# Pooling keys and values on VectorE with one strided reduce, and the keys' second copy on ScalarE

## The chip, the cores and the metric

One core of one Trainium2 chip runs the whole program. The metric is the device time of one execution in microseconds. The engines are named as in the profile: PE is TensorE, DVE VectorE, ACT ScalarE, POOL GpSimd and SP SyncE, whose queue issues the DMAs.

## The reference

Attention in which keys and values are first averaged over groups of eight positions, then two dense blocks with a gate between their matrices:

```python
B, H, S, D = 8, 8, 576, 64          # q, k, v
k_p = k.reshape(B, H, S // 8, 8, D).mean(axis=3)      # 72 pooled keys a head
v_p = v.reshape(B, H, S // 8, 8, D).mean(axis=3)
attn = softmax(q @ k_p.T / sqrt(D))
x = (attn @ v_p) as [B * S, H * D]                    # 4608 tokens of 512
h = x @ w_in;   x = (h * cos(h)) @ w_out              # w_in 512 x 2048
h = x @ w_in2;  out = (h * clip(h + 3, 0, 6) / 6) @ w_out2
```

## The kernel before

The dense blocks run token block by token block (nine blocks of 512), and in each over chunks of 128 hidden columns. Every product is made of three, since both sides are split into a high and a low part (`xh`, `xl`, `wh`, `wl`). PE does `gemm1` (line 175) and `gemm2` (line 237); ACT and DVE evict and apply the gate in between; the weights arrive as 64-bit words and are put together from them on DVE (lines 116 to 128).

Attention goes batch by batch, in units of 128 query rows, and its pieces are woven between the first steps of the dense block: the tables at the top of `tile_kernel` say how many pieces stand behind each step. A scheduler then sets the order of each engine's instructions from the order in which the program is written and from its own costs; engines run their instructions strictly in that order.

A batch's keys and values are loaded into one buffer, `raw`: 128 partitions with 5 rows of 512 words each, a row being one group of eight positions of 64 words (`load_kv`). Keys, values, the next batch's keys and so on take turns in this single buffer, so a load waits until the pooling ahead of it has read the buffer. `pool_kv` sums the eight positions. Line 334 adds halves in place, first 1280 and then 640 elements per partition; line 338 adds the last two quarters into the target, `kp` for keys and `vt` for values. For keys line 338 runs twice, as `kp` holds each pooled key in two copies next to each other. `make_kbd` transposes both copies on PE (lines 348 and 364) and ACT puts the results into a block-diagonal matrix, `kbd` (line 345), against which the scores are made (line 407). `make_v` splits `vt` on ACT and GpSimd (lines 373 to 382).

The table `VD` sends the pooling of the second batch's values to GpSimd; the other fifteen poolings run on DVE. The softmax around them takes DVE too: a maximum (line 416), a subtraction (418), a sum (429) and its reciprocal (430, 431).

Of the kernel before, what the change touches and what calls it, by code (L numbers as in the profile page):

```python
# [12 lines left out]
AF = mybir.ActivationFunctionType  # L13
ALU = mybir.AluOpType
AX = mybir.AxisListType
# [14 lines left out]
def tile_kernel(ctx, tc, q, k, v, wi1, wo1, wi2, wo2, ident_d, mask_d, out):  # L30
    nc = tc.nc
    B, H, S, D = q.shape
# [30 lines left out]
    KC = (H * SP + P - 1) // P  # L63
# [262 lines left out]
    def pool_kv(b, nm, eng, step=KC):  # L326
        kt = ap.tile([P, KC, 2, D], F32, tag="kp", name="kp") if nm == "k" else None
        vt = ap.tile([P, KC, D], F32, tag="vt", name="vt") if nm == "v" else None
        for c in range(0, KC, step):
            t = raw_t[:, c : min(c + step, KC)]  # L330
            w = POOL * D
            while w > 2 * D:
                w //= 2
                eng.tensor_tensor(  # L334
                    out=t[:, :, :w], in0=t[:, :, :w], in1=t[:, :, w : 2 * w], op=ALU.add
                )
            for o in [kt[:, c : min(c + step, KC), e] for e in range(2)] if nm == "k" else [vt[:, c : min(c + step, KC)]]:
                eng.tensor_tensor(out=o, in0=t[:, :, :D], in1=t[:, :, D : 2 * D], op=ALU.add)
        kp[b, nm] = kt if nm == "k" else vt
# [167 lines left out]
    def attention():  # L507
        units = B * NU
        normed = finished = 0
        for n in range(units + 3):  # L510
# [12 lines left out]
            if n < units and b + 1 < B:  # L523
                if i == 2:
                    pool_kv(b + 1, "k", nc.vector if KD[b + 1] else nc.gpsimd)
                    load_kv(b + 1, "v")
                if i == 4:
                    make_kbd(b + 1, 0)
                    yield
                    make_kbd(b + 1, 1)  # L530
                    yield
# [3 lines left out]
            while finished < normed and n - finished >= 2:  # L535
                unit_pt(finished)
                yield
                qb, qi = divmod(finished, NU)
                finished += 1
                if qi in (1, 3):  # L540
                    unit_pt_rest(qb, qi - 1)
                    yield
                for part, (u0, u1) in enumerate(PARTS[qb]):
                    if qi == min(u1 - 1 + (part == 0) * PV0, NU - 1):
                        for j in range(NP):
                            pv(qb, part, j)
                            yield
                        if UNITS[u1 - 1][0] + P >= N:
                            started.append(qb)
                if qi == NU - 1:  # L550
                    done.append(qb)
                    if qb + 1 < B:
                        pool_kv(qb + 1, "v", nc.vector if VD[qb + 1] else nc.gpsimd)
                        make_v(qb + 1)
                        if qb + 2 < B:
                            load_kv(qb + 2, "k")
# [22 lines left out]
    for t in vr.values():  # L579
        nc.gpsimd.memset(f(t), 0.0)  # L580
    pool_kv(0, "k", nc.vector, K0S)
    load_kv(0, "v")
    make_kbd(0, 0)
# [77 lines left out]
    for slot in range(2 * (T + LAG) + 4):  # L661
# [3 lines left out]
        if not odd and s < T:  # L665
# [9 lines left out]
            if key[0] == 1 and fc == NF - 5:  # L675
                for c in range(NC):
                    t = ypl.tile([P, N], F32, tag="yv", name="yv", bufs=4)
                    nc.sync.dma_start(
                        out=t, in_=yp_d[c * P : (c + 1) * P, bl * N : (bl + 1) * N]
# [6 lines left out]
            if nxt < T:  # L686
                nm, nk, nbl = steps[nxt][:3]
# [87 lines left out]
```

## Time and profile before

| | us |
|---|---|
| median of three runs | 1803.48 |
| lowest and highest | 1799.16 and 1804.42 |
| the profiled execution | 1801.62 |
| its span | 1799.8 |
| PE busy in it | 1739.2 (97%) |
| DVE busy | 896.4 (50%) |
| ACT busy | 891.6 (50%) |
| POOL busy | 393.8 (22%) |

A share of busy time is a mean over stages that differ: attention fills roughly the first 440 us, with dense work in it from about 87 us on, and behind it the dense blocks run alone. What a change in attention is worth is read from the stretch in which it lies.

### The profile page before, as it was taken

The page shows a single profiled execution, that of the slowest core. Times are in us where ns is not written, and L with a number is a line of the kernel's source. Part 1 is how long each engine was busy: PE and PEld are TensorE (multiplying, and loading weights), DVE is VectorE, ACT ScalarE, POOL GpSimd, SP SyncE. Part 2 cuts the span into 40 slices and gives each one's busy share as a digit, 9 for nine tenths or more (in the row PEclk, how much of TensorE's full clock was granted, in tenths as well). Part 3 has the DMA queues.
Part 4 walks back from the last instruction along what each step waited for, and adds up shares of the span by engine and source line. Part 5 has one row for each costly group of instructions (what it writes and reads, how often), then busy time and mean ns, then how long its engine had stood idle before and what let it go on. Part 6 is the DMA issues. An engine that isn't in the chain of part 4 may idle for free.

```text
span 1799.8 us, 21002 instructions
## 1 busy us (share of the span) xinstructions
PE 1739.2 (97%) x7952; PEld 1429.5 (79%) x7952; DVE 896.4 (50%) x1398; ACT 891.6 (50%) x1508; POOL 393.8 (22%) x320
## 2 busy tenths in 40 slices
PE   5689999999999999999999999999999999999999
PEld 4567777788888888888888788888888888888887
DVE  6998656656777656654446852222222222222222
ACT  3588878787666655555556543232323222232222
POOL 2755444222223222221112421010101000010000
PEclk7799999999999999999999999999999999999999
DMA  7656442323333313222223411010101010100000
GB/s 196 194 172 195 143 136 74 118 83 103 117 105 118 106 59 105 97 85 76 71 70 106 140 59 47 1 47 1 47 1 48 0 47 8 40 18 24 0 24 24
DMA packets 115077, 139.84 MB, mean 78 GB/s; under 512 B 44192, under 2 KB 68896, under 8 KB 114976
## 3 DMA queue, kind: packets, MB, share of 16 engines
q1 hardware_dynamic: 114976, 138.51, 24.8%
q8 instruction: 62, 1.02, 0.2%
q14 instruction: 39, 0.32, 0.1%
HBM read 100.73 MB, written 37.75 MB: 77 GB/s over the span
## 4 chain that ended last, share of the span: by engine, by line
PE 85%; DVE 6%; DMA 3%; POOL 2%; ACT 2%; issue 2%; SPq 0%; DVEq 0%; POOLq 0%; ACTq 0%
PE y L237 40%; PE h L175 40%; PE ap_ps L494 1%; PE ap_ps L407 1%; DVE raw L334 1%; DMA raw<-in_k_dram 1%; DMA raw<-in_v_dram 1%; POOL xl L153 1%; DVE sm L429 1%; DVE g L196 1%; POOL e L433 1%; DVE a L125 1%; PE ap_ps L393 0%; PE ap_ps L459 0%; DVE sm L430 0%
## 5 line engine op out<-in xcount | busy, mean ns | idle before, releaser
L175 PE MATMUL h<-xl,wh 128*128 128x512 f32 x1152 | 451.3, 392 | 4.2 <-POOL xl L153 4.2
L175 PE MATMUL h<-xh,wh 128*128 128x512 f32 x1152 | 453.5, 394 | 0.5 <-DVE g L209 0.5
L175 PE MATMUL h<-xh,wl 128*128 128x512 f32 x1152 | 450.8, 391 | 0.0
L201 DVE SCALAR_TENSOR_TENSOR g<-g,h 128x512 f32<-128x512 f32 x144 | 99.3, 689 | 454.7 <-ACT g L187 454.7
L153 POOL TENSOR_TENSOR xl<-xr,xh 128x512 fp32r<-128x512 f32 x108 | 153.3, 1438 | 779.2 <-ACT xh L152 778.1
L187 ACT ACTIVATE g<-h,bias_c 128x512 f32<-128x512 f32 x144 | 99.0, 687 | 409.7 <-PE h L175 409.3
L218 DVE TENSOR_TENSOR gl<-g,gh 128x512 fp32r<-128x512 f32 x255 | 190.3, 746 | 157.7 <-ACT gh L212 154.4
L212 ACT ACTIVATE gh<-g 128x512 fp32r<-128x512 f32 x288 | 181.6, 630 | 175.2 <-DVE g L201 104.5
L175 PEld LDWEIGHTS h<-xl,wh 128*128 128x128 f32 x1152 | 216.7, 188 | 50.2 <-POOL xl L153 6.5
L175 PEld LDWEIGHTS h<-xh,wh 128*128 128x128 f32 x1152 | 216.9, 188 | 45.5 <-issue 1.2
L175 PEld LDWEIGHTS h<-xh,wl 128*128 128x128 f32 x1152 | 216.9, 188 | 44.3
L237 PE MATMUL y<-gh,wh 128*128 128x512 f32 x576 | 226.7, 394 | 0.0
L237 PE MATMUL y<-gl,wh 128*128 128x512 f32 x576 | 226.6, 393 | 0.0
L237 PE MATMUL y<-gh,wl 128*128 128x512 f32 x576 | 225.6, 392 | 0.0
L237 PE MATMUL y<-wh,gh 128*128 128x512 f32 x576 | 224.3, 389 | 1.1 <-DVE yv L245 1.1
L237 PE MATMUL y<-wh,gl 128*128 128x512 f32 x576 | 224.1, 389 | 0.0
L237 PE MATMUL y<-wl,gh 128*128 128x512 f32 x576 | 224.1, 389 | 0.0
L196 DVE SCALAR_TENSOR_TENSOR g<-g,t 128x512 f32<-128x512 f32 x144 | 112.6, 783 | 149.8 <-ACT g L195 149.5
L134 POOL TENSOR_TENSOR wl<-a,wh 128x512 fp32r<-128x512 f32 x64 | 88.4, 1381 | 269.4 <-ACT wh L133 269.4
L237 PEld LDWEIGHTS y<-wh,gh 128*128 128x128 f32 x576 | 108.2, 188 | 24.4 <-DVE yv L245 1.9
L199 ACT ACTIVATE g<-g 128x512 f32<-128x512 f32 x144 | 91.0, 632 | 72.9 <-DVE g L196 72.5
L237 PEld LDWEIGHTS y<-wh,gl 128*128 128x128 f32 x576 | 108.1, 188 | 22.5
(110 smaller groups left out, 2086.1 us busy)
## 6 DMA issues: line engine op xcount, KB each, us to landing
xr<-x_d SPq DMA_DIRECT2D x72, 256.0 KB, 3.2
st<-in_moe_w_in_dram SPq DMA_DIRECT2D x32, 512.0 KB, 6.6
st<-in_moe_w_out_dram SPq DMA_DIRECT2D x32, 512.0 KB, 4.1
yp_d<-ys SPq DMA_DIRECT2D x36, 256.0 KB, 2.4
yv<-yp_d SPq DMA_DIRECT2D x36, 256.0 KB, 3.4
xr<-y_d SPq DMA_DIRECT2D x36, 256.0 KB, 2.7
out_dram<-ys SPq DMA_DIRECT2D x36, 256.0 KB, 2.0
raw<-in_k_dram SPq DMA_DIRECT2D x8, 1024.0 KB, 5.7
```

What stands on the lines that cost most here:

```text
L125: nc.vector.scalar_tensor_tensor(out=a, in0=hi, scalar=0xC0000000, in1=a, op0=ALU.bitwise_and, op1=ALU.bitwise_or)
L134: nc.gpsimd.tensor_tensor(out=wl, in0=w, in1=f(wh), op=ALU.subtract)
L153: nc.gpsimd.tensor_tensor(out=xl, in0=t, in1=f(xh), op=ALU.subtract)
L175: nc.tensor.matmul(h, a[:, cs], z, start=(n == 0), stop=(n == 3 * NC - 1))
L187: nc.scalar.activation(out=g, in_=hs[s], func=AF.Relu, bias=bias_c[:, 2:3], scale=1.0)
L196: mark[s] = nc.vector.scalar_tensor_tensor(out=g, in0=g, scalar=MAGIC, in1=t, op0=ALU.subtract, op1=ALU.subtract)
L199: nc.scalar.activation(out=g, in_=g, func=AF.Sin, scale=-TWO_PI)
L201: mark[s] = nc.vector.scalar_tensor_tensor(out=g, in0=g, scalar=6.0, in1=h, op0=ALU.min, op1=ALU.mult)
L212: nc.scalar.activation(out=gh, in_=g, func=AF.Copy)
L218: eng.tensor_tensor(out=gl, in0=gs[s][0], in1=f(gh), op=ALU.subtract)
L237: nc.tensor.matmul(y[c], a, z, start=(first and n == 0), stop=(last and n == 2))
L334: eng.tensor_tensor(out=t[:, :, :w], in0=t[:, :, :w], in1=t[:, :, w : 2 * w], op=ALU.add)
```

## The change

In `pool_kv`, poolings on DVE become one reduce over a view of `raw` in which the eight positions are the innermost dimension. Neighbours in that dimension are 64 words apart. For keys it writes the first copy in `kp`, and ACT copies it to the second. The branch for GpSimd stays as it was. `raw` is no longer written by the pooling. Behind the change line numbers are 8 higher than before.

```diff
         for c in range(0, KC, step):
             t = raw_t[:, c : min(c + step, KC)]
+            if eng is nc.vector:
+                o = kt[:, c : min(c + step, KC), 0] if nm == "k" else vt[:, c : min(c + step, KC)]
+                eng.tensor_reduce(
+                    out=o, in_=t.rearrange("p c (r d) -> p c d r", d=D), op=ALU.add, axis=AX.X
+                )
+                if nm == "k":
+                    nc.scalar.activation(out=kt[:, c : min(c + step, KC), 1], in_=o, func=AF.Copy)
+                continue
             w = POOL * D
             while w > 2 * D:
```

`KC` is 5 and `step` is 5 everywhere, so each pooling is one reduce. The order of instructions changes on all engines through the first 440 us. Three places show how.

On DVE at the start of the program, the first batch's keys and values; before:

```order
L334 TENSOR_TENSOR raw<-raw 128x5x256
L334 TENSOR_TENSOR raw<-raw 128x5x128
L338 TENSOR_TENSOR kp<-raw 128x5x64 x2
L416 TENSOR_REDUCE mx<-ap_ps 128x4 x2
L418 TENSOR_TENSOR e_96<-ap_ps,mx 128x288 x2
L416 TENSOR_REDUCE mx<-ap_ps 128x4
L334 TENSOR_TENSOR raw<-raw 128x5x256
L429 TENSOR_REDUCE sm<-e_96 128x8
L334 TENSOR_TENSOR raw<-raw 128x5x128
L430 TENSOR_SCALAR sm<-sm 128x8
L418 TENSOR_TENSOR e_97<-ap_ps,mx 128x288
L338 TENSOR_TENSOR vt<-raw 128x320
```

The same place after the change:

```order
L333 TENSOR_REDUCE kp<-raw 128x5x64
L424 TENSOR_REDUCE mx<-ap_ps 128x4 x2
L426 TENSOR_TENSOR e_96<-ap_ps,mx 128x288 x2
L333 TENSOR_REDUCE vt<-raw 128x320
L437 TENSOR_REDUCE sm<-e_96 128x8
```

Four instructions for the keys have become one, and three for the values, which had two of the softmax between them, one that runs ahead of the softmax's sum.

On DVE, the pooling of the fourth batch's values, among steps of the softmax and of the gate (`g`); before:

```order
L334 TENSOR_TENSOR raw<-raw 128x5x256
L209 TENSOR_TENSOR g<-h,g 128x512
L334 TENSOR_TENSOR raw<-raw 128x5x128
L429 TENSOR_REDUCE sm<-e_97 128x8
L464 TENSOR_TENSOR ptl<-ap_ps,pth 128x4x128
L430 TENSOR_SCALAR sm<-sm 128x8
L472 TENSOR_TENSOR pth<-ap_ps,pth 64x256
L431 RECIPROCAL sm<-sm 128x8
L338 TENSOR_TENSOR vt<-raw 128x320
```

And after:

```order
L209 TENSOR_TENSOR g<-h,g 128x512
L125 SCALAR_TENSOR_TENSOR a<-st,a 128x512
L116 TENSOR_SCALAR a<-st 128x512
L128 SCALAR_TENSOR_TENSOR a<-e,a 128x512
L437 TENSOR_REDUCE sm<-e_99 128x8
L333 TENSOR_REDUCE vt<-raw 128x320
L438 TENSOR_SCALAR sm<-sm 128x8
L472 TENSOR_TENSOR ptl<-ap_ps,pth 128x4x64
```

The reduce stands in one piece and earlier: at the softmax's sum over `e_99`, where the three sums stood around that over `e_97` (four buffers take turns, so that is two units on). `raw` comes free there.

On ACT, around the third batch's keys; before:

```order
L502 ACTIVATE xs<-y_548 128x320
L379 ACTIVATE vml<-spl,mask 128x4x64
L395 ACTIVATE qT<-ap_ps 128x512
L463 ACTIVATE pth<-ap_ps 128x4x128
L152 ACTIVATE xh<-xr 128x512 x2
L395 ACTIVATE qT<-ap_ps 128x4x64
L423 ACTIVATE e_96<-e_96 128x576
```

And after:

```order
L387 ACTIVATE vml<-spl,mask 128x4x64 x2
L403 ACTIVATE qT<-ap_ps 128x512
L337 ACTIVATE kp<-kp 128x5x64
L510 ACTIVATE xs<-y_542 128x320
L471 ACTIVATE pth<-ap_ps 128x4x128
L403 ACTIVATE qT<-ap_ps 128x4x64
L431 ACTIVATE e_96<-e_96 128x576
```

The copy of the keys (line 337) has come in ahead of an eviction (`xs`), of transposed probabilities (`pth`), of transposed queries (`qT`) and of an exponential, and the copies `xh` have moved behind them.

## Rows read from the trace of the kernel before

**Rows 1.** the page's part 2, PE busy in tenths, 40 slices of 45 us

```profile
PE   5689999999999999999999999999999999999999
```

**Rows 2.** stretches: limits, length, busy of each engine, clock, DMA share, GB/s

```profile
20.00:160.00 140.00, 107.78 (x518) 84.53 (x519) 131.07 (x218) 90.90 (x174) 82.68 (x70) 0.83 0.64 182
160.00:340.00 180.00, 170.57 (x901) 137.09 (x900) 120.49 (x215) 145.07 (x252) 76.81 (x72) 1.00 0.45 137
340.00:440.00 100.00, 98.82 (x528) 80.88 (x527) 58.16 (x117) 83.55 (x143) 28.37 (x27) 1.00 0.23 73
440.00:1800.00 1360.00, 1355.00 (x5977) 1121.08 (x5975) 579.67 (x835) 567.11 (x931) 204.70 (x147) 1.00 0.18 57
```

**Rows 3.** same columns, DVE on `raw` alone, a stretch per pooling; last all

```profile
7.00:11.00 4.00, 3.21 (x4) 1.00 0.99 155
20.00:25.00 5.00, 2.79 (x3) 0.86 0.48 97
32.00:39.00 7.00, 4.21 (x4) 0.50 0.65 147
67.00:73.00 6.00, 4.10 (x4) 0.92 0.83 250
85.00:99.00 14.00, 5.02 (x3) 0.88 0.22 67
111.00:121.00 10.00, 3.60 (x4) 1.00 0.45 127
133.00:141.00 8.00, 4.07 (x3) 1.00 0.44 131
151.00:158.00 7.00, 3.17 (x4) 1.00 0.49 172
...
5.00:345.00 340.00, 54.03 (x53) 0.93 0.54 158
```

**Rows 4.** instructions of four lines: ns min/median/max, first and last start, shapes

```profile
L334 DVE TENSOR_TENSOR raw<-raw x30: 778/1478/2549, 7.4 to 332.5; 128x1280 f32<-128x1280 f32 x15, 128x640 f32<-128x640 f32 x15
...
L429 DVE TENSOR_REDUCE sm<-e x40: 734/748/756, 21.7 to 426.2; 128x8 f32<-128x576 f32 x32, 64x8 f32<-64x576 f32 x8
...
L116 DVE TENSOR_SCALAR a<-st x64: 410/421/1517, 26.2 to 1060.9; 128x512 uint32<-128x512 uint32 x64
...
L373 ACT ACTIVATE sph<-vt x8: 454/462/471, 24.0 to 349.3; 128x320 fp32r<-128x320 f32 x8
```

**Rows 5.** DVE's groups by shape: count, busy us, mean ns, idle before, releasers

```profile
L416 DVE TENSOR_REDUCE mx<-ap_ps 128x4 f32<-128x288 f32 x64 | 28.5, 452 | 28.6 <-PE ap_ps L407 28.2
...
L334 DVE TENSOR_TENSOR raw<-raw 128x1280 f32<-128x1280 f32 x15 | 25.6, 1704 | 11.7 <-DMA raw<-in_k_dram 6.3 <-DMA raw<-in_v_dram 5.4
L429 DVE TENSOR_REDUCE sm<-e 128x8 f32<-128x576 f32 x32 | 24.0, 750 | 23.4 <-ACT e L423 20.3 <-POOL gl L218 3.1
```

**Rows 6.** chain of waits from the start: start, length, what

```profile
7.36 1.50 DVE raw L334
...
8.89 0.83 DVE raw L334
...
9.75 0.91 DVE kp L338 x2
...
11.80 8.40 DMA raw<-in_v_dram
```

**Rows 7.** PE's waits to 170 us: us in total, times, longest

```profile
PE h L348 <- DVE kp L338: 13.2, 2, 10.7
PE ap_ps L407 <- DVE e L418: 10.6, 5, 4.5
```

**Rows 8.** ACT's table loads in the groups by shape

```profile
L199 ACT ACT_TABLE_LOAD x28 | 35.9, 1283 | 0.5
L423 ACT ACT_TABLE_LOAD x27 | 34.6, 1283 | 1.6 <-DVE e L418 1.1
...
L345 ACT ACT_TABLE_LOAD x1 | 1.3, 1283 | 2.4 <-DVE kbd L577 2.4
```

## The prediction

> **What bounds the kernel now.** I read the page's slices first, then the stretches, then the pools one by one. [rows 1] is to show where TensorE (PE) waits: its row is full from the fourth slice on and low only in the first three, which are 45 us each. [rows 2] gives that in numbers: from 440 us to the end PE is busy 1355.0 of 1360 us, so nothing that the change touches can be gained or lost there. PE is idle 32.2 us from 20 to 160, 9.4 us from 160 to 340 and 1.2 us in the 100 us after that. From 20 to 160 us VectorE (DVE) is busy 131.07 of 140 us, more than any other engine. There DVE sets the pace, with GpSimd (POOL, 82.68 us) as the next in its chains. From 160 to 340 us DVE is busy only 120.49 of 180 us and PE 170.57: there most of DVE's work is hidden. The granted TensorE clock is below full only in the DVE-bound stretch (0.83 in the mean), when PE has little to do; I price no term on it, since PE is not what ends late there.
>
> **What the pools cost now.** [rows 3] has one stretch for each pool and only the instructions on the buffer raw. I call them k0, v0, k1 and so on, by batch. k0, v0, k1, k2, v2, k3, v3 and k4 lie ahead of 160 us and take 3.21 + 2.79 + 4.21 + 4.10 + 5.02 + 3.60 + 4.07 + 3.17 = 30.17 us of DVE. All fifteen on DVE take 54.03 us (last row), so the seven later ones 23.86 us. v1 is on GpSimd before and after. The undisturbed price is that of k0, 3.21 us, and v0, 2.79 us. The rest is contention: k0's first sum takes 1.50 us on the chain [rows 6], the slowest 2549 ns [rows 4].
>
> **The new reduce.** One reduce reads all 2560 elements of each partition once. DVE has two reduces in the trace: 288 elements in 452 ns (from PSUM) and 576 in 750 ns (from SBUF) [rows 5]. That is (750 − 452) / 288 = 1.035 ns per element, so 2560 elements would take 0.750 + 1984 × 1.035 ns = 2.80 us. This is the lower end. The reduce of 576 elements stays between 734 and 756 ns in all forty [rows 4], in the same stretches in which the two-input sums swing, so I give the new one no contention of its own. But those reduces read neighbouring words. The new one walks `p c d r`: each next element lies 64 words (256 bytes) away. The widest step of a long DVE read in the trace is 8 bytes, the weights' words at line 116, which run at 421 ns for 512 elements at the median [rows 4]; a wider one has a handful of elements at most, and tells nothing. For the upper end I take the slowest pace at which DVE was seen to read words for this same pooling: 2549 ns for 1280 elements, 1.99 ns each [rows 4], and so 2560 × 1.99 ns = 5.10 us. Below nothing is excluded: an element more per cycle than the rows of reduces show has no row.
>
> Which end? By operation and count the nearest row is the reduce; by what is in doubt, whether a word comes in every cycle, it is the slow sum. I choose the slow end, 5.10 us, as a judgement on the step alone, with somewhat better than even odds.
>
> The Trainium skill (SBUF — State Buffer, section "Door 1: The DMA port swizzle") says that SBUF has lines of 16 bytes, that two accesses must fall in a line for full bandwidth, and that fp32 may step four elements free; this speaks against the change, as no two neighbours of the new read share a line. The trace's 8-byte step agrees and shows nothing of 256 bytes. The page gives no size; if it were a halved pace, an estimate from that page is 0.75 + 1.984 × 2.07 = 4.9 us, about my slow end, and if it costs nothing the sum is that of the first rival.
>
> **Sum at 5.10 us.** Ahead of 160 us: 8 × 5.10 − 30.17 = +10.6 us of DVE work. DVE has just 9 us idle of the 140 there, so it can hide little; against that, parts of the chain run through GpSimd, which a DVE with fewer two-input sums disturbs less. I let 0.8 of it reach the end: +8.5 us. k0 and v0 pass in full, as [rows 6] shows: load, sums, the issue of the next load, that load and v0's sums follow each other on the chain. Later: 7 × 5.10 − 23.86 = +11.8 us, in a stretch where DVE idles a third and PE is 95% busy; I let 0.2 pass: +2.4 us.
>
> **ScalarE's copy.** Eight copies of 320 elements; ScalarE (ACT) copies the same size in 462 ns at the median at line 373 [rows 4], so 3.7 us of ACT work. From k2 on at least fourteen rows of ACT's order lie between a copy and the first use of what is made from it, and ACT is busy 145.07 of 180 us even where it is fullest [rows 2]: nothing. k0 and k1 are bare: PE waits for them at line 348, 10.7 us and 2.5 us (13.2 in two) [rows 7], and now waits for reduce, copy and a hand-over: 0.46 + about 0.1 us each, +1.2 us in all. DVE's second add, 0.48 us, is in the sums above. Only the sine (line 199), the exponential (line 423) and the very first instruction of ACT load a table before [rows 8]; the copy adds none, and the first load moves ahead of k0's copy, under the input's load: nothing.
>
> **What the new order moves.** The scheduler places one reduce near where the first of the three sums stood, so raw comes free and the next load goes out earlier (before, k3's three sums stretch over 10 us, v2's over 14 [rows 3]). DVE waited 11.7 us in all for raw's loads [rows 5], the very first load among it, which stays; what else there is lies mostly behind 200 us, where DVE has time. I count no gain; the most would be 11.7 × 0.2 = 2.3 us. ACT has 52 table loads in the new order against 56. Each takes 1283 ns [rows 8], 5.1 us of ACT work less. ACT is not the bound, but few of its waits are loose; I take a tenth, −0.6 us rounded up, with bounds 0 and −5.1. Everything else that changes places (a sum of softmax, a weight step, a GEMM step a few rows earlier or later) I price at nothing, plus or minus 3 us: a stall of PE behind such a step (scores, line 407, behind the subtraction, line 418) was 2.1 us in the mean and 4.5 at most [rows 7], and they can come or go singly.
>
> Total: 8.5 + 2.4 + 1.2 − 0.6 = +11.5 us. The profiled execution took 1801.62 us (span 1799.8, and 1.8 us around it, which stay), which gives **1813 us**. That execution lies 1.9 us under the median of the three times, 1803.48, and I make no further shift for it. A measurement of this kernel can tell about 0.3% (5.4 us) from no change.
>
> **Rivals.**
> *The reduce runs at full pace (ends on the other side).* Mechanism: DVE reads a word per cycle whatever the step. Price 2.80 us; the point from which it decides is 30.17 / 8 = 3.77 us per pool, below which DVE has less to do in its full stretch. Ahead of 160 us: 8 × 2.80 − 30.17 = −7.8 us, of which I let only 0.6 pass, since POOL and the loads take over as what is late: −4.7. Later: 7 × 2.80 − 23.86 = −4.3 us × 0.2 = −0.9. With the copy and the tables: 1801.6 − 4.7 − 0.9 + 1.2 − 0.6 = 1797 us. For it speaks that both reduces run at one element per cycle and a steady time; against it the step that they do not have.
>
> *ACT is held up by its copies.* ACT runs in order, and the copy waits for DVE's reduce at a place that was chosen ahead of time. Behind k2's copy stand the eviction xs, the transposed probabilities pth, qT and an exponential, all of which feed PE. If DVE is late by some 2 us at five of the seven copies that is up to 10 us, of which half may reach PE. At full pace this takes back the gain: 1797 + 5 = 1802 us; on the slow price it makes 1818. For it: DVE has no slack before 160 us. Against: only k2, k3 and k4 have their copies there.
>
> *The change does next to nothing*: the price is near 3.8 us per pool, and DVE's sum stays. 1801 to 1803 us. A pace of 1.4 ns per element would do that; no row points to it.
>
> **How the numbers follow.** Slow reduce 0.57: its own range is 1804 to 1824 us, the upper end with all 22.4 us passing (1801.6 + 22.4 + 1.2 − 0.6 = 1825, rounded down), the lower with a fifth of the early work and none of the later. Of it 0.49 is slower by over 0.3%, 0.08 within. Full pace 0.25: 1790 to 1800, of it 0.15 faster, 0.10 within. ACT held up 0.10: 1799 to 1819, of it 0.06 slower, 0.04 within. Next to nothing 0.08: 0.04 within, 0.02 to either side, for the order. Together: faster 0.17, same 0.26, slower 0.57. The range goes from 1794 to 1824: it takes in most of the full-pace case, and leaves out some 0.1 below and less above.
>
> **What would show it.** Mean of the new DVE group at line 333: near 5.1 or near 2.8 us. DVE's busy sum: +22 us at the slow price (less the contention that goes), −12 us at the full one. k0's last sum ends at 10.66 us now [rows 6]: PE's first matmul on kp 2.5 us later than that, or within 0.3 us. If the reduce is slow and the time still falls, the share that passes is wrong, and the early stretch was not DVE's. If it is fast and the time does not fall, the next thing late (POOL, the loads, ACT's copies) has taken the gain, and PE's waits will name it.

## The result, and the profile after

The changed kernel takes 1825.54 us in the median of four runs (1822.3 to 1826.16), the kernel before 1801.69 us in four. The ratio is 1.0134, with a 95% interval of 1.0121 to 1.0146: 1.3% slower, some 24 us. The sign was forecast; the size was about twice the +11.5 us of the sum, and the time lies just above the range.

From the page of the changed kernel, busy times of the engines, PE's slices as in [rows 1], and the granted clock by slices:

```profile
PE 1747.2 (96%) x7952; PEld 1436.4 (79%) x7952; DVE 918.4 (50%) x1360; ACT 890.1 (49%) x1512; POOL 384.2 (21%) x320
...
PE   4687899999999999999999999999999999999999
...
PEclk8789999999999999999999999999999999999999
```

PE's busy time went from 1739.2 to 1747.2 us for the same 7952 matmuls, and its idle time from 60.6 to 77.1 us (span 1824.3 less busy time). So 16.5 us of the span's 24.5 are new idle time, and 8.0 us are the same work done more slowly. This division holds for these two traces only: e7 below takes the same time as the changed kernel with PE busy 1741.4 us.

The stretches that answer to [rows 2], same columns:

```profile
20.00:160.00 140.00, 103.19 (x484) 81.05 (x483) 132.57 (x192) 84.85 (x168) 75.19 (x67) 0.80 0.62 179
160.00:340.00 180.00, 162.68 (x837) 130.95 (x836) 121.33 (x182) 131.82 (x233) 68.81 (x69) 0.97 0.39 119
340.00:440.00 100.00, 95.92 (x503) 78.76 (x502) 61.23 (x113) 80.52 (x136) 27.16 (x26) 0.98 0.27 86
440.00:1800.00 1360.00, 1358.32 (x6014) 1123.38 (x6013) 589.96 (x855) 582.48 (x960) 211.86 (x153) 1.00 0.18 59
```

PE is idle 36.8 us from 20 to 160 us (32.2 before), 17.3 us from 160 to 340 (9.4) and 4.1 us from 340 to 440 (1.2). DVE's share is hardly higher anywhere: it is busy 121.33 of 180 us in the later stretch, a third idle as before. The granted clock, full in both later stretches before, is now 0.97 and 0.98.

The new group at line 333, in ns min/median/max with first and last start, and DVE's whole busy time on `raw` (columns as in [rows 3]):

```profile
L333 DVE TENSOR_REDUCE kp<-raw x8: 4452/4702/4812, 7.0 to 331.7; 128x320 f32<-128x2560 f32 x8
L333 DVE TENSOR_REDUCE vt<-raw x7: 4479/4648/4726, 21.8 to 353.6; 128x320 f32<-128x2560 f32 x7
```

```profile
5.00:375.00 370.00, 69.85 (x15) 0.91 0.50 146
```

One reduce takes 4.45 to 4.81 us. The fifteen take 69.85 us against 54.03 [rows 3]: +15.8 us of DVE, and 24 us of time.

### The profile page after: what moved, and what is told of

Same layout as the page of the kernel before. It is cut to its first block, busy times and chain, and to the rows that moved or that the text cites. A ratio compares the mean times of both kernels' runs of the same rounds, so it can differ in the third digit from the quotient of the medians.

```text
span 1824.3 us, 20961 instructions
## 1 busy us (share of the span) xinstructions
PE 1747.2 (96%) x7952; PEld 1436.4 (79%) x7952; DVE 918.4 (50%) x1360; ACT 890.1 (49%) x1512; POOL 384.2 (21%) x320
## 4 chain that ended last, share of the span: by engine, by line
PE 84%; DVE 8%; ACT 3%; issue 2%; DMA 1%; POOL 1%; SPq 0%; DVEq 0%; ACTq 0%; POOLq 0%
PE h L175 40%; PE y L237 40%; PE ap_ps L502 2%; DVE kp L333 2%; PE ap_ps L415 1%; DMA raw<-in_v_dram 1%; DVE vt L333 1%; DVE sm L437 1%; ACT L431 1%; DVE a L125 1%; DVE a L128 1%; PE ap_ps L401 1%; DVE sm L438 0%; DVE g L196 0%; DVE ptl L472 0%
## 5 line engine op out<-in xcount | busy, mean ns | idle before, releaser
L237 PEld LDWEIGHTS y<-wh,gh 128*128 128x128 f32 x576 | 108.2, 188 | 24.3 <-DVE yv L245 1.9
L237 PEld LDWEIGHTS y<-gh,wh 128*128 128x128 f32 x576 | 109.0, 189 | 22.1 <-ACT ys L253 0.5
```

Of the source, the lines that this page charges most:

```text
L237: nc.tensor.matmul(y[c], a, z, start=(first and n == 0), stop=(last and n == 2))
```

## The experiments

Theory A: the step of the read makes the reduce dear, and its extra time reaches the end wherever it lies. Rivals: the new order and the copies queued on ACT (B), the 320 short outputs (C), the length of one block on DVE (D). Each ratio is to the kernel before on the same chip; a difference of two ratios times 1800 us gives microseconds, good to about 3 us each.

**e1: the same order, neighbouring words.**

```diff
-                    out=o, in_=t.rearrange("p c (r d) -> p c d r", d=D), op=ALU.add, axis=AX.X
+                    out=o, in_=t.rearrange("p c (d r) -> p c d r", d=D), op=ALU.add, axis=AX.X
```

> The changed kernel with one thing altered: the reduce sums eight neighbouring words instead of eight words 256 bytes apart, so it pools the wrong elements. Every engine's order of instructions is exactly that of the changed kernel. Theory A (the step of the read is the cost, and it reaches the end): one reduce takes 2.8 us instead of 4.65, DVE has 28 us less to do than in the changed kernel, and the time is 1795 to 1803 us. Theory B (the new order and the copy's waits on ACT are most of the loss): the reduce takes 2.8 us too, but the time stays above 1808 us. Theory C (the 320 short outputs are the cost, not the step): the reduce stays at 4.6 us and the time at 1825 us.

Measured: 1796.51 us, ratio 0.998 (0.9971 to 0.999). DVE's groups in e1 by shape (busy us, mean ns, idle before):

```profile
L333 DVE TENSOR_REDUCE kp<-raw 128x320 f32<-128x2560 f32 x8 | 22.5, 2814 | 7.4 <-DMA raw<-in_k_dram 4.2 <-PE ap_ps L372 3.2
L333 DVE TENSOR_REDUCE vt<-raw 128x320 f32<-128x2560 f32 x7 | 19.7, 2817 | 5.4 <-DMA raw<-in_v_dram 4.1 <-issue 1.3
```

C falls: the outputs are the same and a reduce takes 2.82 us. B falls too, as the main cause: with this very order, and with the copies where they are, the kernel is 0.2% faster than before. From e1 to the changed kernel nothing differs but the step, and the traces have the same order of instructions on every engine; the step costs 15 × 1.85 = 27.6 us on DVE (69.85 against 42.2 us) and (1.0134 − 0.998) × 1800 = 27.7 us of time.

**e2: one duration for each step.**

```diff
+                st = {2: 1, 3: 2, 4: 4, 5: 8, 6: 16, 7: 32}.get(b)
+                if nm == "v" and st is not None:
+                    eng.tensor_reduce(
+                        out=vt.rearrange("p c d -> p (c d)").rearrange("p (x s) -> p x s", s=st),
+                        in_=raw_t.rearrange("p c e -> p (c e)").rearrange("p (x r s) -> p x s r", r=POOL, s=st),
+                        op=ALU.add, axis=AX.X,
+                    )
+                else:
```

> The changed kernel, in which the values of batches 2 to 7 are reduced with steps of 1, 2, 4, 8, 16 and 32 words (4 to 128 bytes) instead of 64, so those sums are of the wrong elements; keys and the first values keep 64. One duration for each step, all for 2560 elements into 320. A line of 16 bytes as the limit: 2.8 us at 1 and 2 words, 4.65 us from 4 words on, and nothing in between. A cost that grows with the step: durations rise from 2.8 towards 4.65 us over the six. No effect of the step: all near 4.65 us.

Measured in a single execution, 1823.22 us. The six reduces of e2 in order of time, so with steps of 1, 2, 4, 8, 16 and 32 words (start, us, shapes):

```profile
94.07 2.80 DVE L335 TENSOR_REDUCE vt<-raw 128x320 f32<-128x2560 f32 x1
...
123.38 2.81 DVE L335 TENSOR_REDUCE vt<-raw 128x320 f32<-128x2560 f32 x1
...
172.04 4.71 DVE L335 TENSOR_REDUCE vt<-raw 128x320 f32<-128x2560 f32 x1
...
223.95 4.84 DVE L335 TENSOR_REDUCE vt<-raw 128x320 f32<-128x2560 f32 x1 [1.81 <-DMA raw<-in_v_dram]
...
279.83 4.54 DVE L335 TENSOR_REDUCE vt<-raw 128x320 f32<-128x2560 f32 x1 [0.47 <-DMA raw<-in_v_dram]
...
350.47 4.78 DVE L335 TENSOR_REDUCE vt<-raw 128x320 f32<-128x2560 f32 x1 [0.52 <-DMA raw<-in_v_dram]
```

2.80 and 2.81 us at steps of 4 and 8 bytes, 4.54 to 4.84 us at 16 to 128 bytes, and no duration in between. It is a threshold between 8 and 16 bytes, not a slope; 12 bytes was not run. The Trainium skill (SBUF — State Buffer, section "Door 1: The DMA port swizzle") puts the limit at a line of 16 bytes with at least two hits in it. The runs agree with that: a step of 8 bytes leaves two hits in a line, a step of 16 only one. The same passage says that fp32 may step four elements free. That is not borne out here if it means a step of four, which takes 4.71 us.

**e3: the copy alone.** Pairwise sums as before; only the second copy goes to ACT.

```diff
-            for o in [kt[:, c : min(c + step, KC), e] for e in range(2)] if nm == "k" else [vt[:, c : min(c + step, KC)]]:
-                eng.tensor_tensor(out=o, in0=t[:, :, :D], in1=t[:, :, D : 2 * D], op=ALU.add)
+            o = kt[:, c : min(c + step, KC), 0] if nm == "k" else vt[:, c : min(c + step, KC)]
+            eng.tensor_tensor(out=o, in0=t[:, :, :D], in1=t[:, :, D : 2 * D], op=ALU.add)
+            if nm == "k":
+                nc.scalar.activation(out=kt[:, c : min(c + step, KC), 1], in_=o, func=AF.Copy)
```

> One half of the change alone: the pairwise sums stay as in the kernel before, but the keys' second copy is made by ACT. Theory A (the reduce's price is the loss): within 3 us of the kernel before, or up to 5 us faster, as DVE has 8 x 0.48 to 0.6 us less to do. Theory B (ACT held up by the copies): 5 to 12 us slower than the kernel before.

Measured: 1800.25 us, ratio 1.0005 (0.9995 to 1.0014). DVE on `raw` in e3 (the first columns as in [rows 3]; one memset of half a microsecond is among the 46):

```profile
0.00:345.00 345.00, 50.20 (x46) 0.94 0.54 159
```

DVE has about 4 us less to do, and the time does not move. The copy on ACT, with the add that it replaces on DVE, is neither a gain nor a loss.

**e7: the change, with DVE's own copy.**

```diff
-                    nc.scalar.activation(out=kt[:, c : min(c + step, KC), 1], in_=o, func=AF.Copy)
+                    nc.vector.tensor_copy(out=kt[:, c : min(c + step, KC), 1], in_=o)
```

> The changed kernel, but the keys' second copy is made by DVE behind its reduce, as in the kernel before; the step stays 256 bytes. Order changes slightly. If ACT's copies, queued behind the late reduces, carry part of the loss: 3 to 10 us faster than the changed kernel. If the reduce alone does: the same, or up to 5 us slower for eight more DVE instructions of about 0.4 us in the full stretch, 1825 to 1831 us.

Measured: 1826.16 us, ratio 1.015 (1.0135 to 1.0165). In e7, DVE's groups:

```profile
L333 DVE TENSOR_REDUCE kp<-raw 128x320 f32<-128x2560 f32 x8 | 37.5, 4686 | 10.9 <-PE ap_ps L372 6.4 <-DMA raw<-in_k_dram 4.5
...
L337 DVE COPY kp<-kp 128x320 f32<-128x320 f32 x8 | 2.8, 347 | 0.0
```

With 2.8 us more on DVE and no copy on ACT it is as slow as the changed kernel: ACT's copies carry nothing of the loss that shows within some 3 us.

**e5 and e6: the step early or late, in the same order.** The view is the strided one for `b < 4` in e5 and for `b >= 4` in e6, and neighbouring words otherwise.

> In the changed kernel's exact order, keys and values of batches 0 to 3 are reduced at the 256-byte step, the eight reduces of batches 4 to 7 over neighbouring words (wrong elements). Seven reduces cost 7 x 1.85 = 13.0 us more of DVE than with all of them over neighbouring words (1796.5 us). Theory A (all of it reaches the end, wherever it lies): 1808 to 1811 us. The prediction's shares (0.8 of the early work, 0.2 of the late): 1806 to 1808 us.

> The reverse, in the same order: batches 4 to 7 at the 256-byte step, batches 0 to 3 over neighbouring words (wrong elements). Eight reduces cost 8 x 1.85 = 14.8 us more of DVE, in stretches where DVE is busy two thirds of the time. Theory A (all of it reaches the end): 1809 to 1814 us. The prediction's share of 0.2 for the late stretch: 1799 to 1801 us. If neither kernel's loss adds up with the other's to 29 us, the two meet in a wait that both lengthen.

Measured: e5 1808.5 us, ratio 1.0049 (1.0034 to 1.0064); e6 1812.93 us, ratio 1.0075 (1.0058 to 1.0092). Against e1's ratio, e5 loses (1.0049 − 0.998) × 1800 = 12.4 us for 13.0 us of DVE work, e6 17.1 us for 14.8. Together 29.5 us, as much as the whole step costs within the errors: the two add. The early share is 0.95, where 0.8 was forecast; the late share is not 0.2 but about 1 (1.15, good to 0.2).

**e10: only the late values.**

```diff
-                    out=o, in_=t.rearrange("p c (r d) -> p c d r", d=D), op=ALU.add, axis=AX.X
+                    out=o, in_=t.rearrange("p c (r d) -> p c d r" if b >= 4 and nm == "v" else "p c (d r) -> p c d r", d=D), op=ALU.add, axis=AX.X
```

> The changed kernel's exact order; the 256-byte step only for the values of batches 4 to 7, neighbouring words (wrong elements) for all else: 4 x 1.85 = 7.4 us more of DVE than with neighbouring words throughout (1796.5 us). If every late reduce costs alike: 1804 to 1805 us, half of the 16.4 us that the eight cost. If the values' reduces, which stand between the softmax's maximum and the subtraction that frees the scores, carry most of it: 1806 to 1810 us. If the keys' do: below 1802 us.

Measured: 1807.76 us, ratio 1.0046 (1.0031 to 1.0061): (1.0046 − 0.998) × 1800 = 11.9 us for 4 × 1.85 = 7.4 us of DVE. Late values lose more than they take. The late keys were not run alone; 17.1 − 11.9 = 5.2 us are left for their equal 7.4, which the errors don't tell from all of it.

The place shows in the trace. DVE in the changed kernel around the fifth batch's values (start, us, line; idle before and releaser in brackets), and PE at the same time:

```profile
222.07 0.46 DVE L424 TENSOR_REDUCE mx<-ap_ps 128x4 f32<-128x288 f32 x1 [0.99 <-PE ap_ps L415]
224.63 4.54 DVE L333 TENSOR_REDUCE vt<-raw 128x320 f32<-128x2560 f32 x1 [2.10 <-DMA raw<-in_v_dram]
229.10 0.45 DVE L426 TENSOR_TENSOR e<-ap_ps,mx 128x288 f32<-128x288 f32 x1
```

```profile
225.62 0.39 PE L237 MATMUL y<-gh,wl 128*128 128x512 f32 x1
229.65 1.08 PE L401 MATMUL ap_ps<-ident,qm 128*128 128x128 f32 x4 [3.64 <-issue]
```

And in e1, DVE and PE at the same place of the program:

```profile
203.99 0.46 DVE L424 TENSOR_REDUCE mx<-ap_ps 128x4 f32<-128x288 f32 x1 [1.00 <-PE ap_ps L415]
206.58 2.82 DVE L333 TENSOR_REDUCE vt<-raw 128x320 f32<-128x2560 f32 x1 [2.14 <-DMA raw<-in_v_dram]
209.32 0.45 DVE L426 TENSOR_TENSOR e<-ap_ps,mx 128x288 f32<-128x288 f32 x1
```

```profile
207.51 0.39 PE L237 MATMUL y<-gh,wl 128*128 128x512 f32 x1
209.87 0.63 PE L401 MATMUL ap_ps<-ident,qm 128*128 128x128 f32 x4 [1.97 <-issue]
```

DVE waits 2.10 us for the load with the subtraction of line 426 queued behind the reduce. PE has 3.7 us of other matmuls behind the scores, to 226.0 us, and then runs dry; its transposes of line 401 start 0.10 us after the subtraction has ended (229.10 + 0.45, then 229.65; in e1 209.32 + 0.45, then 209.87). The trace names no releaser for them, so that they wait for the scores' buffer which this subtraction reads is inferred: from the equal 0.10 us, and from the kernel, which has two `ap_ps` buffers here, both taken by the two halves of the scores. PE stands 3.64 us with the step and 1.97 us without, 1.67 us apart for a reduce that is 1.72 us longer. PE's waits of this kind from 160 to 360 us (total, times, longest), in e10 and then in e1:

```profile
PE ap_ps L401 <- issue: 7.3, 3, 3.3
```

```profile
PE ap_ps L401 <- issue: 2.7, 2, 2.0
```

Then the clock. Four stretches of 4 us in the changed kernel around that stall, with one of 1 us listed last, and three in e1 around its own (columns as in [rows 2], granted clock third from the end):

```profile
222.00:226.00 4.00, 4.00 (x20) 3.06 (x19) 1.82 (x2) 0.89 (x2) 1.29 (x1) 1.00 0.22 76
226.00:230.00 4.00, 0.36 (x3) 0.39 (x3) 3.97 (x4) 0.63 (x1) 0.00 (x0) 0.93 0.01 2
230.00:234.00 4.00, 4.00 (x18) 3.49 (x17) 1.61 (x3) 3.19 (x4) 0.00 (x0) 0.65 0.92 279
234.00:238.00 4.00, 4.00 (x20) 3.31 (x19) 2.25 (x6) 3.30 (x7) 2.69 (x3) 1.00 0.40 88
...
230.00:231.00 1.00, 1.00 (x6) 0.90 (x5) 1.00 (x2) 0.23 (x1) 0.00 (x0) 0.50 0.62 68
```

```profile
203.50:207.50 4.00, 4.00 (x22) 3.40 (x21) 1.38 (x2) 0.40 (x2) 1.28 (x1) 1.00 0.20 59
207.50:211.50 4.00, 2.03 (x15) 1.42 (x14) 3.69 (x5) 1.93 (x4) 0.00 (x0) 1.00 0.19 35
211.50:215.50 4.00, 4.00 (x20) 3.30 (x19) 1.52 (x4) 3.96 (x6) 0.98 (x1) 1.00 1.06 331
```

Behind the stall of 3.64 us, in which PE did 0.36 us of work in 4 us, the granted clock falls: it reads 0.50 at first, the lower level of 1.2 GHz, and 0.65 over the next 4 us is a mix of that with the full 2.4 GHz, while in e1, with a stall of 1.97 us, it stays at full. So the step costs 1.7 us of stall at this place and, by estimate, 4 × (1 − 0.65) = 1.4 us of slow matmuls behind it. From 160 to 440 us in e1, e6 and e10:

```profile
160.00:440.00 280.00, 269.59 (x1430) 218.75 (x1429) 174.34 (x311) 224.96 (x391) 95.69 (x94) 1.00 0.35 109
```

```profile
160.00:440.00 280.00, 259.55 (x1358) 209.96 (x1357) 180.41 (x300) 213.38 (x368) 93.20 (x92) 0.98 0.32 98
```

```profile
160.00:440.00 280.00, 263.28 (x1378) 213.44 (x1377) 177.91 (x301) 217.66 (x376) 95.39 (x95) 0.98 0.33 101
```

PE is idle 10.4 us in e1, 20.4 in e6 and 16.7 in e10; the clock of 0.98 in the other two takes, by estimate, another 280 × 0.02 = 5.6 us, good to 1.4 us since the clock is rounded. That makes some 15.6 us for e6 (17.1 measured) and 11.9 for e10 (11.9, closer than the estimate can claim).

**e4, e8 and e9: five pieces.** Each reduce becomes five, between which the scheduler may put other work; e8 is the same order over neighbouring words, e9 takes the step for `b >= 4` alone.

```diff
+                for i in range(KC):
                     eng.tensor_reduce(
-                        out=o, in_=t.rearrange("p c (r d) -> p c d r", d=D), op=ALU.add, axis=AX.X
+                        out=o[:, i], in_=t[:, i].rearrange("p (r d) -> p d r", d=D), op=ALU.add, axis=AX.X
                     )
```

> The changed kernel with each reduce split into five, one for each row of 512 words, so that the scheduler may put other work between them; the read step stays 256 bytes. Theory D (a 4.65 us block on DVE stalls what stands behind it, beyond its work): 5 to 12 us faster than the changed kernel, though DVE's work grows by the fixed cost of four more instructions a pooling, about 0.1 us each. Theory A (the work alone counts): the same or up to 6 us slower than the changed kernel, 1825 to 1832 us.

> The kernel of five pieces with the read step taken away: neighbouring words are summed (wrong elements), in exactly that kernel's order. A piece of 512 elements should fall from 1.05 to about 0.69 us, 75 x 0.36 = 27 us less of DVE, the same saving as between the changed kernel and its contiguous form, which moved the time by 29 us. Theory A (DVE's work passes in full, in whatever portions): 1788 to 1792 us. Theory D (part of the 29 us came from the length of the block, and in short pieces DVE's work is partly hidden): a smaller share, 15 to 21 us, 1796 to 1802 us.

> The kernel of five pieces in its exact order, with the 256-byte step only for batches 4 to 7 and neighbouring words (wrong elements) for batches 0 to 3. It puts a number on the late work when other work can go between the pieces: 40 pieces, 40 x 0.375 = 15.0 us more of DVE than with all pieces over neighbouring words (1795.4 us). With blocks of 4.65 us the same late work cost 16.4 us. Theory A (late work passes in any portion): 1809 to 1812 us. Theory D (the length of the block matters late): 1801 to 1806 us. The prediction's 0.2: 1798 us.

Measured: e4 1816.9 us, ratio 1.0093 (1.0078 to 1.0108); e8 1795.42 us, ratio 0.9969 (0.9958 to 0.9981); e9 1805.11 us, ratio 1.0033 (1.0022 to 1.0044). The pieces in e4, then in e8:

```profile
L334 DVE TENSOR_REDUCE kp<-raw 128x64 f32<-128x512 f32 x40 | 40.6, 1050 | 8.1 <-PE ap_ps L373 4.1 <-DMA raw<-in_k_dram 4.0
...
L334 DVE TENSOR_REDUCE vt<-raw 128x64 f32<-128x512 f32 x35 | 35.5, 1048 | 3.8 <-DMA raw<-in_v_dram 3.8
```

```profile
L334 DVE TENSOR_REDUCE kp<-raw 128x64 f32<-128x512 f32 x40 | 25.5, 673 | 7.7 <-DMA raw<-in_k_dram 3.9 <-PE ap_ps L373 3.8
...
L334 DVE TENSOR_REDUCE vt<-raw 128x64 f32<-128x512 f32 x35 | 22.6, 676 | 6.8 <-DMA raw<-in_v_dram 6.8
```

e4 has some 6 us more on DVE than the changed kernel and is 0.4 of a percent faster: the length of the block matters, as D had it. From e8 to e4 the step costs 75 × 0.37 = 28 us of DVE and (1.0093 − 0.9969) × 1800 = 22 us of time, a share of 0.8, between what A and D expected; e8's median missed both ranges. Late alone, e9, it is 11.5 us for 15.0, where whole blocks lost 17.1 for 14.8. PE's stalls at the transposes (line 402 there) are nearly gone in e9, where e6 has 7.8 us; more of its waiting is now for ACT ahead of the scores:

```profile
PE ap_ps L416 <- ACT xs L511: 4.7, 4, 2.6
...
PE ap_ps L402 <- issue: 1.1, 2, 0.9
```

So A is right for most of the work, and D for some of the rest: the 5.6 us between e6 and e9 go with the length of the block, and with another order, and are hardly more than the errors.

## Why the prediction was right and wrong

- **The sign, and its cause:** right. The step of the read is the cost, shown by e1 and e2, and the choice between the two ends fell on the right one.
- **The price:** 5.10 us forecast from the slowest sum in [rows 4], 4.66 us measured (69.85 / 15). This term was 0.44 us too dear a pooling, and the pooling's growth on DVE +15.8 us instead of +22.4. That it came so close is in part luck: the row was a sum over neighbouring words, which takes 1.50 us elsewhere [rows 6], so its slowness was not that of a step. DVE's busy sum on the page did grow by 22.0 us (896.4 to 918.4), the sign that the prediction had named, but only 15.8 of them are pooling.
- **The price and the shares together:** two errors worked against each other. With the measured price the prediction's terms are 8 × 4.66 − 30.17 = +7.1 us early and 7 × 4.66 − 23.86 = +8.8 us late, and its shares, copy and tables make that +8.0 us. Even with both shares at 1 it is +16.5 us, where +24 was measured. The range's upper end let all of DVE's growth pass; more than all of it did.
- **The full-pace rival:** 2.80 us a reduce and 1797 us were forecast; e1 has 2.82 us and 1796.51 us. The slope from the two reduces of [rows 5] was good to 1%, and so was the absence of contention.
- **The early share, 0.8:** a little low. e5 passes 12.4 of 13.0 us, and its 1808.5 us lie in the range of theory A, half a microsecond above that of the prediction's shares (its seven reduces are those of `b < 4`; the sum counted an eighth, k4, ahead of 160 us, which is in e6).
- **The late share, 0.2:** the step that failed. It was read from busy shares ([rows 2]: DVE idle a third of the stretch, PE 95% busy), as though DVE's idle time could take the work. It can't: e6 shows 17.1 us lost for 14.8, so late work was worth some five times what the sum gave it. Of DVE's 59.5 us idle from 160 to 340 us in the kernel before, 46.5 are waits for ACT and PE, and ACT in its turn waits 9.7 us there for DVE (lines 209 and 196): the engines hand work round a loop. DVE's waits (us, times, longest):

```profile
DVE g L196 <- ACT g L195: 12.8, 8, 3.7
DVE sm L429 <- ACT e L423: 12.1, 9, 2.2
DVE g L209 <- ACT g L199: 11.4, 12, 2.8
DVE mx L416 <- PE ap_ps L407: 10.2, 11, 2.6
```

And at the place shown above PE had 3.7 us of other work to go on with, less than the wait for the load and the reduce together.
- **The clock, priced at nothing:** wrong for the late stretch. [rows 2] has it at full there; it comes down behind longer stalls (e1 against e10). Summed over stretches of 1 us, PE's busy time multiplied by what the clock lacks is 19.4 us up to 160 us and nothing from there to 460 us in the kernel before, 21.1 and 6.5 us in the changed one: so by this estimate most of the 8.0 us that PE's busy time grew by is late.
- **ScalarE's copy:** priced +1.2 us for two bare waits. The first rose from 10.7 [rows 7] to 12.0 us, reduce and copy together, where a first matmul 2.5 us after 10.66 had been forecast; the two waits together stay at 13.2:

```profile
PE h L356 <- ACT kp L337: 13.2, 2, 12.0
```

- **ACT held up by its copies:** it cost nothing that shows. ACT does stand 16.0 us for the reduces, ahead of five of its eight copies and 9.5 of them at the start, but e3 and e7 show no price for it. What was held up was DVE's own queue, by the reduce; the prediction had looked for a queue behind the wait on ACT and not behind the reduce.
- **The new order:** −0.6 us for the table loads and nothing else, plus or minus 3. In e1 the order, the copies and a reduce of 2.82 us together make −3.4 us against the 1799.9 us of the kernel before, where the rival's sum had −5.0. No run has the order alone, so that it is worth nothing isn't shown.
- **The old sums, taken as worth what the new work is worth:** the sum priced only the difference of the two, and this too failed. The step's 27.6 us on DVE cost 27.7 us of time; the 11.8 us that go from DVE between the kernel before and e1 (54.03 to 42.2 us) gave back 3.4 us. So 27.7 − 3.4 = 24.3 us are lost, for a difference on DVE of 15.8. Why the old sums were worth so little stays open. They may have been partly hidden, as three or four short instructions a pooling; or the new order costs up to some 8 us. Two runs speak for the first without showing it. e8, in pieces, has 5.9 us more on DVE than e1 and is no slower (0.9969 against 0.998). And e3, with the old sums, has DVE's busy time from 20 to 160 us down from 131.07 [rows 2] to 123.96 us, and gains nothing:

```profile
20.00:160.00 140.00, 109.33 (x536) 87.36 (x536) 123.96 (x215) 94.00 (x181) 86.72 (x71) 0.84 0.65 187
```

Left open, too: how much of a late stall would stay if the reduce stood behind the subtraction instead of ahead of it; no kernel moved it alone. No version that computes the reference was faster than the kernel before: e3 is equal to it, and e1 and e8, which are 0.2 and 0.3% faster, add neighbouring words in place of the eight rows.

## What to carry to other kernels

Count the read step of a VectorE instruction as part of its price: an fp32 reduce over a view that steps 256 bytes took 1.66 times what it took over neighbouring words, and from 16 bytes on it was about as dear. The pairwise sums over neighbouring words, 3.6 us a pooling (54.03 / 15), were cheaper than one such reduce of 4.66 us. An engine that is busy two thirds of a stretch isn't thereby able to hide more work: look at what stands behind the longer instruction on its queue, and how many microseconds of other work the engine that waits for it has in hand. Don't price a change by the difference of old and new work on one engine alone: 11.8 us less gave 3.4 us here, 27.6 us more cost 27.7. Two kernels in exactly the same order, with the one price changed, told in a single run what the step was worth, and what all the rest was worth together.

## What the runs showed of the hardware

The cost of the step is one threshold, between 8 and 16 bytes: 2.80 and 2.81 us for 2560 fp32 elements at 4 and 8 bytes, 4.71, 4.84, 4.54 and 4.78 us at 16 to 128 bytes, and 4.45 to 4.81 at 256. From pieces of 512 and wholes of 2560 elements that is (4657 − 1049) / 2048 = 1.76 ns per element at the large step and (2815 − 675) / 2048 = 1.04 ns at the small, so 1.7 times and not twice. Over neighbouring words the reduce's time hardly moved, 2.80 to 2.82 us for all fifteen in e1, where the two-input sums of 1280 elements that they replace had reached 2549 ns [rows 4]. And the granted clock stayed at full through a stall of PE of 1.97 us and fell, to 0.50 at first and 0.65 over 4 us, behind one of 3.64 us at the same place.
